# Key sums on halves of TensorE's columns, and a new ranking in a hand-made planner: linear attention and two MLPs on one core

## The chip, the cores and the metric

The kernel runs on one core of a Trainium2 chip. The metric is the device time of one execution in microseconds. The measurement of the kernel before is the median of 3 runs, 954.39 us (953.98 to 955.47).

## The reference, cut to what matters

The inputs are q, k, v of shape (4 batches, 8 heads, 576 tokens, 64), omega of 128 x 64, and the weights of two MLPs (512 to 2048 and back).

```python
def phi(x):
    h = x @ omega.T - sum(x * x) / 2
    return exp(h - max(h)) / sqrt(128)
q_p, k_p = phi(q * 64**-0.25), phi(k * 64**-0.25)
kv = einsum('bhsm,bhsd->bhmd', k_p, v)          # the key sums
z = sum(k_p, axis=2)
out = (q_p @ kv) / (q_p @ z + 1e-6)             # per batch and head
x = out as (2304 tokens, 512)
h = x @ w_in;  g = max(h, 0) + alpha * min(h, 0);  x = g @ w_out
h = x @ w2_in; g = 0 if h <= -1, h if h >= 1, else (h + 1)**2 / 4;  out = g @ w2_out
```

All of it is float32.

## The kernel before, in words

**Attention.** The 32 heads are worked on as 16 pairs of two heads of one batch. 576 tokens are 4 tiles of 128 (NJ = 4) and 64 last tokens, and the last tokens of both heads of a pair share one tile. For a pair, `features` (L344) multiplies keys and then queries with omega: a head has 64 features of input, so that the two heads use the two halves of TensorE's rows (L361). `last_features` (L367) does the last tokens (L373). `exponentials` (L329) takes the maximum on VectorE (L336) and 128 x 128 exponentials on ScalarE (L339). `key_sums` (L377) multiplies the keys' features with the values and a column of ones: one matmul for the last tokens with 130 moving columns (L388), then eight with 65 (L395), all into one PSUM bank; each float32 matmul is two passes in the trace. `transposed` (L432) transposes the queries' features, `quotients` (L467) multiplies them with the key sums (L473, or three products for pairs from 6 on), and `back` (L490) divides (L482 to L523) and writes x, the MLP's input.

**MLPs.** Tokens stand in four groups: one batch of 512 main tokens each, and in the fourth the 256 last tokens of all batches too. For each MLP, each group and each of 16 blocks of 128 hidden features there is a unit: 2 x 4 x 16 = 128 units in a row. A unit multiplies x with the first weights into a bank h (`hidden`, L673), applies the activation (`activate`, L644: L652 and L653 in the first MLP, L656 to L658 in the second) and multiplies with the second weights into the banks y (`project`, L682). Every product is three matmuls (L243 to L245) of a rounded part and a rest: `hi_of` (L225, ScalarE or VectorE) makes the rounded part, `lo_of` (L232) subtracts it. So the weights have a split for each unit (`split_weights`, L300: w_hi on ScalarE, w_lo on GpSimd), x one for each group (`split_x`, L626: x_hi and x_lo, 512 wide for main tokens and 256 wide for the last ones) and g one for each unit (L664, L665). The order of TensorE is: hidden of unit i + 1, then project of unit i.

**Words.** The weights come as 64-bit numbers. `convert` (L253) loads 512 KB into a word buffer (three of them, L251 and L257) and makes float32 in five steps on ScalarE, GpSimd and VectorE (L265 to L273). The first MLP's weights are converted during group 0, at most five units ahead; those of the second from the time when attention has given back its memory (`attended`, L608, event "late").

**What sets the order.** Nothing is scheduled by a compiler. `Plan` (L38) runs all streams in a simulated time when the kernel is built: each step names an engine and a charge in ns, and the planner emits the step that can start first; among those that start at the same time, the one of the lowest rank:

```python
return (start, s.pe_rank if engine == "pe" else s.rank, s.ready), engine, ns, emit
```

Each engine then executes in that order, and semaphores do the waiting. A rank decides only between steps that could start at the same time. Before, attention has rank 3 plus its batch (and ranks below 0 on TensorE), conversions of the first MLP 4.5, of the second 20, splits of weights 3.5, the MLPs, activations, x's splits and `finish` 0, and loads of attention's inputs about -100. `mlps` (L737) adds x's splits of the next group, all of them, with the first unit of a group; they wait there until x's parts are free (main tokens: when the last unit has used them; last tokens: these are used by group 3 alone).

Of the kernel before, what the change touches and what calls it, by code (L numbers as in the profile page):

```python
# [11 lines left out]
U32 = mybir.dt.uint32  # L12
# [134 lines left out]


def _pool_one(n, emit, handicap=0.0):
    return "pool", 80 + n, emit, handicap  # L150


def _pe(ns, emit):
    return "pe", ns, emit
# [7 lines left out]
def favor_attention_two_mlps(  # L162
# [20 lines left out]
    nc = tc.nc  # L183
# [13 lines left out]
    NE = NF // 2  # L197
    AHEAD = 5
    N_FULL = 6
    WARM = 18  # L200
    ROWS_NS = 264

    const = ctx.enter_context(tc.tile_pool(name="const", bufs=1))
    wpool = ctx.enter_context(tc.tile_pool(name="w", bufs=NF))
# [6 lines left out]

    plan = Plan()
    events = {}

    def ev(*key):
        return events.setdefault(key, Event())

    def done(*key):
        plan.set(ev(*key))
# [28 lines left out]
        return 3 * max(109.0, 13.5 + n / 2.4)  # L248


    raws = Tokens([0, 1, 2])  # L251

    def convert(dst, src, key):  # L253

        n = dst.shape[1]
        yield raws
        raw = stage_p.tile([P, 2 * n], U32, tag="raw", name="raw", bufs=3)  # L257
        yield _dma(P * n * 8, lambda: nc.sync.dma_start(raw, src))
        f = raw.bitcast(F32).rearrange("p (n t) -> p n t", t=2)[:, :, 1]
        h = raw.bitcast(U16).rearrange("p (n t) -> p n t", t=4)[:, :, 1]  # L260
        low, e = (raw.rearrange("p (n t) -> p n t", t=2)[:, :, t] for t in range(2))
        d = dst.bitcast(U32)

        yield [
            _act(n, lambda: nc.scalar.activation(f, f, AF.Copy, scale=2.0**-112)),  # L265
            _pool_one(n, lambda: nc.gpsimd.tensor_scalar(f, f, 2.0**-112, 0.0, ALU.mult, ALU.add), 300),
        ]
        yield _act(n, lambda: nc.scalar.activation(low, h, AF.Copy, scale=2.0**-13))
        yield _dve_fast(n, lambda: nc.vector.tensor_scalar(d, e, 3, None, ALU.logical_shift_left))  # L269
        yield _pool(n, lambda: nc.gpsimd.tensor_tensor(d, d, low, ALU.add))  # L270
        yield _dve_two(
            n,
            lambda: nc.vector.scalar_tensor_tensor(  # L273
                d, e, 0x80000000, d, ALU.bitwise_and, ALU.bitwise_or
            ),
        )
        plan.put(raws, 0)
        done("w", *key)
# [4 lines left out]
    def load_weights(l, src):  # L283
        for f in range(NF):
            if l == 0:
                yield ev("unit", f - AHEAD)
            if l == 1 and f < NE:
                yield ev("late")
                w = late["pool"].tile([P, 2, DM], F32, tag="w", name="w2", bufs=NE)
            else:  # L290
                yield w_slots
                w = wpool.tile([P, 2, DM], F32, tag="w", name="w")
            weights[l, f] = w
            for a in range(2):
                plan.add(convert(w[:, a, :], src[f, :, a * 2 * DM : (a + 1) * 2 * DM], (l, f, a)), (4.5, 20)[l])

    part_slots = [Tokens([0, 1]) for _ in range(2)]
    parts = {}
# [1 line left out]
    def split_weights(a):  # L300
        for i, (l, g, f) in enumerate(units):
            yield part_slots[a]
            yield ev("w", l, f, a)
            w = weights[l, f][:, a, :]
            hi = parts_p.tile([P, DM], F32R, tag=f"wh{a}", name="w_hi")
            lo = parts_p.tile([P, DM], F32R, tag=f"wl{a}", name="w_lo")
            yield hi_of(hi, w, 3000)
            yield lo_of(lo, w, hi, ("pool",))
            parts[i, a] = hi, lo
            done("part", i, a)  # L310
            if l == 0 and g == len(groups) - 1:
                if ev("split", f).at is not None:
                    plan.put(w_slots, 0)
                done("split", f)


    free_banks = Tokens(["y0", "y1", "y2", "y3", "a0", "a1"])
# [59 lines left out]
    def key_sums(pool, kf, lf, vm, vl, pair):  # L377
        for key in ("k0", "k1", "l"):
            yield ev(key, pair)
        yield kv_slots  # L380
        kv_hi = pool.tile([M, 2, 2 * D], F32R, tag="kvh", name="kv_hi", bufs=2)
        kv_lo = pool.tile([M, 2, 2 * D], F32R, tag="kvl", name="kv_lo", bufs=2)
        kvs[pair] = kv_hi, kv_lo
        tag = yield free_banks
        kv = bank(tag)

        def products():
            nc.tensor.matmul(  # L388
                kv[:, : 2 * (D + 1)], lf[:, 0, :], vl.rearrange("p h d -> p (h d)"), start=True, stop=False
            )  # L390
            for h in range(2):
                o = kv[:, h * (D + 1) : (h + 1) * (D + 1)]
                for j in range(NJ):
                    end = h == 1 and j == NJ - 1
                    nc.tensor.matmul(o, kf[:, 2 * j + h, :], vm[:, h, j, :], start=False, stop=end)  # L395

        yield _pe(216 * (2 * NJ + 1), products)
        plan.put(k_slot, 0)
        plan.put(v_slots, 0)
        if pair + 2 < B * NP:  # L400
            plan.add(load_values(pair + 2), pair - 97.5)
        done("kv sums", pair)

        kv3 = kv[:, : 2 * (D + 1)].rearrange("m (h d) -> m h d", h=2)
        z_hi, z_lo = (
            a.rearrange("m h d -> m (h d)")[:, D : 3 * D].rearrange("m (h d) -> m h d", h=2)
            for a in (kv_hi, kv_lo)
        )
        z = kv3[:, :, D : D + 1].to_broadcast([M, 2, D])
        cs = [slice(h * D, (h + 1) * D) for h in range(2)]  # L410

        one = pair < N_FULL

        def his():
            for h in range(2):
                o = kv_hi[:, h, cs[h]]
                nc.scalar.activation(o.bitcast(F32) if one else o, kv3[:, h, :D], AF.Copy)
            nc.scalar.activation(z_hi.bitcast(F32) if one else z_hi, z, AF.Copy)

        def los():  # L420
            for h in range(2):
                o = kv_hi[:, h, cs[h]].bitcast(F32)
                nc.vector.tensor_tensor(kv_lo[:, h, cs[h]], kv3[:, h, :D], o, ALU.subtract)
            nc.vector.tensor_tensor(z_lo, z, z_hi.bitcast(F32), ALU.subtract)

        yield "act", 370, his
        if not one:
            yield "dve", 472, los
        give(tag)
        done("kv", pair)  # L430
# [36 lines left out]
    def quotients(kv_hi, kv_lo, qh, ql, den, num, i, h, pair):  # L467
# [11 lines left out]
        done("n", pair, i, h)  # L479
        own, other = (slice(0, D), slice(D, 2 * D))[:: 1 - 2 * h]  # L480

        yield _dve(SH, lambda: nc.vector.transpose(den[own, c], n[other, :SH]))  # L482
        yield [
            _act(SH, lambda: nc.scalar.copy(num[own, c], n[own, :SH]), 0),
            _dve(SH, lambda: nc.vector.tensor_copy(num[own, c], n[own, :SH]), 50),
# [4 lines left out]
    def back(pool, qh, ql, b, hp, pair):  # L490
# [6 lines left out]
        num = pool.tile([P, S], F32, tag="num", name="num")  # L497
        for i in range(2):
            for h in range(2):
                plan.add(quotients(kv_hi, kv_lo, qh, ql, den, num, i, h, pair), 3 + b, b - 7)  # L500
        for i in range(2):
            for h in range(2):
                yield ev("den", pair, i, h)
# [5 lines left out]
            nc.vector.tensor_scalar(inv, squares[:, :, 0], EPS, None, ALU.add)  # L509
            nc.vector.reciprocal(inv, inv)  # L510

        yield "dve", 130 + 7.3 * NS, invert
        spread = inv.unsqueeze(2).to_broadcast([P, NS, 32])
        yield _dve(S, lambda: nc.vector.transpose(squares, spread))
        ends = [
            (x[b][:, hp, :], num[:, :SM], den[:, :SM]),
            (x[B][:, hp, b * SL : (b + 1) * SL], num[:, SM:], den[:, SM:]),
# [38 lines left out]
    def attend(pool):  # L556
        for pair in range(B * NP):
            b, hp = divmod(pair, NP)
            r = (3 + b, b - 7)
            yield ev("kq", pair, -1 if pair == 0 else 0)  # L560
            yield split_slot
            xt, vm, vl = loaded.pop(pair)
# [174 lines left out]
    def mlps():  # L737
        ys = {}
        for i in range(-1, NU):
            if i + 1 < NU:  # L740
                l, g, f = units[i + 1]
                if f == 0:
                    n = i + 1 + NF
                    if n < NU:
                        nl, ng, _ = units[n]
                        for b in groups[ng]:
                            for c in range(KC):
                                plan.add(split_x(nl, b, c), 0)
                    if l == 0:
                        for b in groups[g]:  # L750
                            plan.add(second_input(b), 0)
                yield ev("part", i + 1, 0)
                for b in groups[g]:
                    tag = yield h_banks
                    h = bank(tag)
                    for c in range(KC):
                        yield ev("xs", l, b, c)
                        yield hidden(i + 1, b, c, h)
                        if f == NF - 1:
                            plan.put(xs_slots[b // B, c], 0)  # L760
                    plan.add(activate(i + 1, b, h, tag), 0)
                plan.put(part_slots[0], 0)
            if i < 0:
                continue
# [10 lines left out]
            for b in groups[g]:  # L775
# [4 lines left out]
                for c in range(n // P if l else KC):  # L780
# [3 lines left out]
                    y, tag = ys[b, c // per]  # L784
                    yield project(i, b, c, y)
                    if f == NF - 1 and c % per == per - 1:
                        plan.add(finish(l, b, c, y, tag, tokens), 0)
                plan.put(g_slots[k], 0)
                gs.pop((i, b))
            plan.put(part_slots[1], 0)  # L790
# [51 lines left out]
    def setup():  # L842
        yield "act", 300, constants

    plan.add(setup(), 0)
    plan.add(load(alpha_sb, alpha, ("alpha",)), 0)
    for f in range(-AHEAD, 0):
        done("unit", f)
    plan.add(attend(pool), 3, -10)
    plan.add(attended(), 0)  # L850
    for l in range(2):
        plan.add(load_weights(l, (w1, w2)[l]), (4.5, 20)[l])
    for a in range(2):
        plan.add(split_weights(a), 3.5)
    for b in groups[0]:
        for c in range(KC):
            plan.add(split_x(0, b, c), 0)
    plan.add(mlps(), 0)
    plan.run()

# [46 lines left out]
```

## Time and profile before

| | |
|---|---|
| median of 3 runs | 954.39 us |
| the profiled execution | 956.27 us |
| its span, first to last instruction | 954.4 us |
| TensorE busy | 931.8 us (98%) |
| VectorE busy | 557.9 us (58%) |
| ScalarE busy | 515.8 us (54%) |
| GpSimd busy | 453.6 us (48%) |
| mean granted TensorE clock | 0.995 |

PE is TensorE, PEld its weight loads, DVE VectorE, ACT ScalarE, POOL GpSimd, SP SyncE. The span of the profiled execution is 1.87 us less than its time. Matmuls overlap in the trace: what a matmul costs in a row of matmuls is the distance of two starts, not its own duration. "L395" is line 395 of the kernel; lines 225 to 245 are helpers, where the names of the tiles tell who called.

### The profile page before, as it was taken

How to read it: one execution, taken by the hardware profiler on the slowest of the kernel's cores; microseconds unless marked ns; L12 is line 12 of the kernel's file. 1: busy time of each engine (PE TensorE's matmuls, PEld its weight loads, DVE VectorE, ACT ScalarE, POOL GpSimd, SP SyncE). 2: the span in 40 equal slices, each digit the busy share in tenths (PEclk: the TensorE clock that was granted, in tenths of full speed). 3: DMA queues.
4: the chain of work that ended last, by engine and by line, in shares of the span. 5: the costliest groups of instructions: out<-in, count | busy, mean ns of one | idle time of the engine just before them, and what ended most of it. 6: DMA issues, size and time to landing. Idle time of an engine off the chain costs nothing.

```text
span 954.4 us, 13551 instructions
## 1 busy us (share of the span) xinstructions
PE 931.8 (98%) x4908; PEld 776.5 (81%) x4908; DVE 557.9 (58%) x944; ACT 515.8 (54%) x1102; POOL 453.6 (48%) x375
## 2 busy tenths in 40 slices
PE   7898999999999999999999999999999999999997
PEld 6677877788888888888888888888887888888886
DVE  4899878885655777777753533453336334534342
ACT  6987777765555654654432354454445445533443
POOL 0544657653333587756743344444443444333330
PEclk9999999999999999999999999999999999999999
DMA  6544434411300023303300000010001000100002
GB/s 184 165 142 131 150 124 155 148 38 38 104 1 1 1 97 116 114 28 133 133 23 1 1 1 1 1 45 0 1 1 45 1 0 1 45 1 1 1 1 66
DMA packets 33858, 53.36 MB, mean 56 GB/s; under 512 B 20992, under 2 KB 21120, under 8 KB 33792
## 3 DMA queue, kind: packets, MB, share of 16 engines
q1 hardware_dynamic: 33632, 52.45, 16.7%
q8 instruction: 38, 0.62, 0.3%
q14 instruction: 28, 0.23, 0.1%
q10 hardware_dynamic: 160, 0.07, 0.0%
HBM read 47.78 MB, written 4.72 MB: 55 GB/s over the span
## 4 chain that ended last, share of the span: by engine, by line
PE 88%; DVE 6%; ACT 4%; issue 1%; DMA 0%; POOL 0%; ACTq 0%; DVEq 0%; POOLq 0%
PE h L243 13%; PE h L245 13%; PE h L244 13%; PE y L243 12%; PE y L245 12%; PE y L244 12%; PE a L243 2%; PE a L361 2%; PE a L245 2%; PE a L244 2%; PE a L395 2%; DVE nm L336 1%; PE a L443 1%; ACT kf L339 1%; DVE x_lo L237 1%
## 5 line engine op out<-in xcount | busy, mean ns | idle before, releaser
L238 POOL TENSOR_TENSOR w_lo<-w,w_hi 128x512 fp32r<-128x512 f32 x256 | 335.2, 1311 | 383.2 <-ACT w_hi L227 379.8
L227 ACT ACTIVATE w_hi<-w 128x512 fp32r<-128x512 f32 x256 | 161.6, 632 | 219.4 <-PE h L244 152.1
L243 PE MATMUL h<-x_hi,w_hi 128*128 128x512 f32 (+1 forms) x640 | 240.3, 376 | 0.0
L245 PE MATMUL h<-x_hi,w_lo 128*128 128x512 f32 (+1 forms) x640 | 236.4, 369 | 0.8 <-POOL w_lo L238 0.8
L244 PE MATMUL h<-x_lo,w_hi 128*128 128x512 f32 (+1 forms) x640 | 236.7, 370 | 0.0
L245 PEld LDWEIGHTS h<-x_hi,w_lo 128*128 128x128 f32 x640 | 121.0, 189 | 22.1 <-POOL w_lo L238 1.5
L243 PEld LDWEIGHTS h<-x_hi,w_hi 128*128 128x128 f32 x640 | 121.2, 189 | 21.7 <-DVE g_lo L236 0.4
L244 PEld LDWEIGHTS h<-x_lo,w_hi 128*128 128x128 f32 x640 | 121.1, 189 | 19.7 <-DVE x_lo L237 0.5
L227 ACT ACTIVATE g_hi<-h 128x512 fp32r<-128x512 f32 (+1 forms) x160 | 89.0, 556 | 83.1 <-DVE h L658 46.6
L236 DVE TENSOR_TENSOR g_lo<-h,g_hi 128x512 fp32r<-128x512 f32 (+1 forms) x160 | 100.2, 634 | 52.0 <-ACT g_hi L227 49.8
L656 DVE TENSOR_SCALAR t<-h 128x512 f32<-128x512 f32 x80 | 51.0, 638 | 135.3 <-PE h L245 133.2
L270 POOL TENSOR_TENSOR w<-w,raw 128x512 uint32<-128x512 uint32 x64 | 85.8, 1343 | 52.9 <-DVE w L269 19.2
L243 PE MATMUL y<-g_hi,w_hi 128*128 128x512 f32 x256 | 103.0, 402 | 0.1
L245 PE MATMUL y<-w_hi,g_lo 128*128 128x512 f32 x256 | 100.2, 391 | 2.3 <-DVE g_lo L236 2.3
L243 PE MATMUL y<-w_hi,g_hi 128*128 128x512 f32 x256 | 100.3, 392 | 0.0
L244 PE MATMUL y<-w_lo,g_hi 128*128 128x512 f32 x256 | 100.3, 392 | 0.0
L244 PE MATMUL y<-g_lo,w_hi 128*128 128x512 f32 x256 | 100.1, 391 | 0.0
L245 PE MATMUL y<-g_hi,w_lo 128*128 128x512 f32 x256 | 100.0, 391 | 0.0
L652 DVE TENSOR_SCALAR t<-h,alpha_sb 128x512 f32<-128x512 f32 x80 | 55.6, 694 | 64.7 <-PE h L245 63.0
L657 ACT ACTIVATE t<-t,half 128x512 f32<-128x512 f32 x80 | 54.5, 681 | 62.1 <-DVE t L656 62.1
L658 DVE TENSOR_TENSOR h<-h,t 128x512 f32<-128x512 f32 x80 | 51.5, 644 | 49.5 <-ACT t L657 49.5
L273 DVE SCALAR_TENSOR_TENSOR w<-raw,w 128x512 uint32<-128x512 uint32 x64 | 59.0, 928 | 8.8 <-POOL w L270 8.7
(115 smaller groups left out, 1308.0 us busy)
## 6 DMA issues: line engine op xcount, KB each, us to landing
raw<-w SPq DMA_DIRECT2D x64, 512.0 KB, 3.7
kq<-kq SPq DMA_DIRECT2D x15, 576.0 KB, 4.6
vm<-v SPq DMA_DIRECT2D x16, 256.0 KB, 3.0
out<-x SPq DMA_DIRECT2D x16, 256.0 KB, 2.0
vl<-v SPq DMA_DIRECT2D x32, 16.0 KB, 2.7
out<-x SPq DMA_DIRECT2D x4, 128.0 KB, 2.3
kq<-kq SPq DMA_DIRECT2D x1, 320.0 KB, 3.1
kq<-kq SPq DMA_DIRECT2D x1, 256.0 KB, 2.7
```

Of the source, the lines that this page charges most:

```text
L227: ops = [_act(n, lambda: nc.scalar.activation(hi, src, AF.Copy))]
L236: "dve": _dve(n, lambda: nc.vector.tensor_tensor(*args), bias),
L238: "pool": _pool(n, lambda: nc.gpsimd.tensor_tensor(*args)),
L243: nc.tensor.matmul(out_, wh, mh, start=first, stop=False)
L244: nc.tensor.matmul(out_, wh, ml, start=False, stop=False)
L245: nc.tensor.matmul(out_, wl, mh, start=False, stop=last)
L270: yield _pool(n, lambda: nc.gpsimd.tensor_tensor(d, d, low, ALU.add))
L273: lambda: nc.vector.scalar_tensor_tensor(d, e, 0x80000000, d, ALU.bitwise_and, ALU.bitwise_or),
L652: yield _dve(n, lambda: nc.vector.tensor_scalar(tn, hn, 0.0, a, ALU.min, ALU.mult))
L656: yield _dve(n, lambda: nc.vector.tensor_scalar(tn, hn, -1.0, 1.0, ALU.max, ALU.min))
L657: yield _act(n, lambda: nc.scalar.activation(tn, tn, AF.Square, bias=half[:, 0:1], scale=0.5), 50)
L658: yield _dve(n, lambda: nc.vector.tensor_tensor(hn, hn, tn, ALU.max))
```

## The change

Six things, of which the diff is the core:

- The key sums' matmuls write 64 of the 128 features each: twice as many matmuls, with stationary tiles of 64 columns, and both halves in turn. The planner charges 1480 ns for a pair in place of 1944.
- The word buffers are four in place of three.
- Ranks: x's splits, activations, `finish` and the constants get -10. Attention gets the number of the unit by which it is due, conversions and weight splits that of the unit which needs them. A weight's split is a stream of its own.
- x's splits of the last tokens are added with the ninth unit of the group before, in place of the first.
- Charges: the projections 298 ns in place of 264 per tile, the transposes of `quotients` and `back` and the inverse a fixed 508, 710 and 480 ns in place of 367, 670 and 261, and L266's alternative on GpSimd 60 ns more.
- On TensorE attention's rank is the pair less 50, in place of the batch less 7.

```diff
-    return "pool", 80 + n, emit, handicap
+    return "pool", 140 + n, emit, handicap
...
+    RAWS = 4
     WARM = 18
-    ROWS_NS = 264
+    ROWS_NS = 298
+    KV_NS = 1480
...
+    URGENT = -10
+
+    def attention_rank(pair):
+        b, hp = divmod(pair, NP)
+        return hp - 8 if b == 0 else NF * (b - 1) + NF // NP * (hp + 1)
+
+    def weight_rank(i):
+        return i - 5.5 if i < 2 else i
...
-    raws = Tokens([0, 1, 2])
+    raws = Tokens(range(RAWS))
...
-                plan.add(convert(w[:, a, :], src[f, :, a * 2 * DM : (a + 1) * 2 * DM], (l, f, a)), (4.5, 20)[l])
+                i = l * len(groups) * NF + f
+                plan.add(convert(w[:, a, :], src[f, :, a * 2 * DM : (a + 1) * 2 * DM], (l, f, a)), weight_rank(i))
...
+            plan.add(split_weight(a, i, weights[l, f][:, a, :], hi, lo), weight_rank(i) - 0.1)
...
-            nc.tensor.matmul(
-                kv[:, : 2 * (D + 1)], lf[:, 0, :], vl.rearrange("p h d -> p (h d)"), start=True, stop=False
-            )
+            halves = [slice(i * M // 2, (i + 1) * M // 2) for i in range(2)]
+            for r in halves:
+                o = kv[r, : 2 * (D + 1)]
+                nc.tensor.matmul(o, lf[:, 0, r], vl.rearrange("p h d -> p (h d)"), start=True, stop=False)
             for h in range(2):
-                o = kv[:, h * (D + 1) : (h + 1) * (D + 1)]
                 for j in range(NJ):
                     end = h == 1 and j == NJ - 1
-                    nc.tensor.matmul(o, kf[:, 2 * j + h, :], vm[:, h, j, :], start=False, stop=end)
-
-        yield _pe(216 * (2 * NJ + 1), products)
+                    for r in halves:
+                        o = kv[r, h * (D + 1) : (h + 1) * (D + 1)]
+                        nc.tensor.matmul(o, kf[:, 2 * j + h, r], vm[:, h, j, :], start=False, stop=end)
+
+        yield _pe(KV_NS, products)
...
-        yield _dve(SH, lambda: nc.vector.transpose(den[own, c], n[other, :SH]))
+        yield "dve", 508, lambda: nc.vector.transpose(den[own, c], n[other, :SH])
...
-                plan.add(quotients(kv_hi, kv_lo, qh, ql, den, num, i, h, pair), 3 + b, b - 7)
+                plan.add(quotients(kv_hi, kv_lo, qh, ql, den, num, i, h, pair), attention_rank(pair), pair - 50)
...
-            r = (3 + b, b - 7)
+            r = (attention_rank(pair), pair - 50)
...
+                n = i + 1 + NF
+                if f in (0, NF // 2) and n < NU:
+                    nl, ng, _ = units[n]
+                    for b in groups[ng]:
+
+                        if (f == 0) == (b < B):
+                            for c in range(KC):
+                                plan.add(split_x(nl, b, c), URGENT)
                 if f == 0:
-                    n = i + 1 + NF
-                    if n < NU:
-                        nl, ng, _ = units[n]
-                        for b in groups[ng]:
-                            for c in range(KC):
-                                plan.add(split_x(nl, b, c), 0)
...
-                    plan.add(activate(i + 1, b, h, tag), 0)
+                    plan.add(activate(i + 1, b, h, tag), URGENT)
...
-                        plan.add(finish(l, b, c, y, tag, tokens), 0)
+                        plan.add(finish(l, b, c, y, tag, tokens), URGENT)
```

## Rows read from the trace of the kernel before

**Rows 1.** The page's first part: busy us and share of the span.

```profile
PE 931.8 (98%) x4908; PEld 776.5 (81%) x4908; DVE 557.9 (58%) x944; ACT 515.8 (54%) x1102; POOL 453.6 (48%) x375
```

**Rows 2.** Stretches: length, busy time by engine (instructions), granted clock, DMA share, GB/s.

```profile
0.00:58.00 58.00, 49.00 (x390) 39.00 (x390) 37.99 (x80) 46.20 (x147) 20.13 (x32) 0.97 0.57 166
58.00:205.00 147.00, 140.81 (x833) 114.00 (x832) 124.86 (x230) 107.80 (x282) 87.14 (x71) 0.99 0.41 135
...
547.00:720.00 173.00, 173.00 (x771) 143.49 (x771) 71.92 (x103) 85.54 (x138) 81.78 (x63) 1.00 0.02 7
720.00:735.00 15.00, 12.66 (x49) 9.94 (x48) 11.53 (x18) 7.28 (x14) 5.15 (x4) 0.89 0.19 72
```

**Rows 3.** Timeline of PE at 725 us: start, us, instruction [idle before <-releaser].

```profile
725.58 0.39 PE L244 MATMUL y<-w_lo,g_hi 128*128 128x512 f32 x1
728.30 0.50 PE L245 MATMUL y<-w_hi,g_lo 128*128 128x512 f32 x1 [2.34 <-DVE g_lo L236]
```

**Rows 4.** Timeline of DVE, 721 to 728 us.

```profile
721.74 1.45 DVE L237 TENSOR_TENSOR x_lo<-x,x_hi 128x512 fp32r<-128x512 f32 x1
...
723.71 1.53 DVE L229 CAST x_hi<-x 128x256 fp32r<-128x256 f32 x2
725.16 2.48 DVE L237 TENSOR_TENSOR x_lo<-x,x_hi 128x256 fp32r<-128x256 f32 x4
727.57 0.68 DVE L236 TENSOR_TENSOR g_lo<-h,g_hi 128x512 fp32r<-128x512 f32 x1
```

**Rows 5.** The chain that ended last, after the hole: start, us on it.

```profile
729.52 0.42 PE y L243
...
732.50 0.43 PE h L244
```

**Rows 6.** Timeline of DVE one group earlier.

```profile
634.70 1.45 DVE L237 TENSOR_TENSOR x_lo<-x,x_hi 128x512 fp32r<-128x512 f32 x1
...
637.43 0.69 DVE L236 TENSOR_TENSOR g_lo<-h,g_hi 128x512 fp32r<-128x512 f32 x1 [0.67 <-ACT g_hi L227]
```

**Rows 7.** Timeline of DVE in the middle of group 2, second MLP.

```profile
773.36 0.69 DVE L656 TENSOR_SCALAR t<-h 128x512 f32<-128x512 f32 x1 [1.84 <-PE h L245]
774.90 0.70 DVE L658 TENSOR_TENSOR h<-h,t 128x512 f32<-128x512 f32 x1 [0.85 <-ACT t L657]
```

**Rows 8.** The chain that ended last, one pair's key sums (pair 14).

```profile
275.36 0.23 PE a L388 x2
275.59 1.73 PE a L395 x16
277.32 0.18 PE a L243
```

**Rows 9.** Timeline of PE around one L361 group in halves of the rows.

```profile
262.33 0.40 PE L245 MATMUL h<-x_hi,w_lo 128*128 128x512 f32 x1
262.65 1.16 PE L361 MATMUL a<-om,kq 64*128 64x128 f32 x16
...
264.08 0.39 PE L244 MATMUL h<-x_lo,w_hi 128*128 128x512 f32 x1
```

**Rows 10.** The chain that ended last, early: a pair's key sums.

```profile
22.70 1.73 PE a L395 x16
```

**Rows 11.** Waits of PE between 58 and 205 us, first and last of seven.

```profile
PE a L361 <- ACT kf L339: 1.8, 1, 1.8
...
PE y L473 <- DVE num L485: 0.3, 1, 0.3
```

**Rows 12.** Timeline of POOL: the last product of pair 7.

```profile
125.33 0.33 POOL L523 TENSOR_TENSOR x<-num,den 128x64 f32<-128x64 f32 x1
```

**Rows 13.** Timeline of PE: the first matmul of group 1, first MLP.

```profile
204.66 0.39 PE L243 MATMUL h<-x_hi,w_hi 128*128 128x512 f32 x1
```

**Rows 14.** Timeline of POOL: the last product of the last pair.

```profile
321.99 0.32 POOL L523 TENSOR_TENSOR x<-num,den 128x64 f32<-128x64 f32 x1
```

**Rows 15.** Timeline of PE: the first matmul of group 3, first MLP.

```profile
414.25 0.39 PE L243 MATMUL h<-x_hi,w_hi 128*128 128x512 f32 x1
```

More of the change, by code (lines that the diff above doesn't have):

```diff
@@ L256, in convert @@
         yield raws
-        raw = stage_p.tile([P, 2 * n], U32, tag="raw", name="raw", bufs=3)
+        raw = stage_p.tile([P, 2 * n], U32, tag="raw", name="raw", bufs=RAWS)
         yield _dma(P * n * 8, lambda: nc.sync.dma_start(raw, src))
@@ L303, in split_weights, with split_weight @@
             yield ev("w", l, f, a)
-            w = weights[l, f][:, a, :]
             hi = parts_p.tile([P, DM], F32R, tag=f"wh{a}", name="w_hi")
             lo = parts_p.tile([P, DM], F32R, tag=f"wl{a}", name="w_lo")
-            yield hi_of(hi, w, 3000)
-            yield lo_of(lo, w, hi, ("pool",))
             parts[i, a] = hi, lo
[L310 to L314, printed above, removed]
+            plan.add(split_weight(a, i, weights[l, f][:, a, :], hi, lo), weight_rank(i) - 0.1)
+    def split_weight(a, i, w, hi, lo):
+        l, g, f = units[i]
+        yield hi_of(hi, w, 3000)
+        yield lo_of(lo, w, hi, ("pool",))
+        done("part", i, a)
+        if l == 0 and g == len(groups) - 1:
+            if ev("split", f).at is not None:
+                plan.put(w_slots, 0)
+            done("split", f)
     free_banks = Tokens(["y0", "y1", "y2", "y3", "a0", "a1"])
@@ L510, in invert @@
             nc.vector.reciprocal(inv, inv)
-        yield "dve", 130 + 7.3 * NS, invert
+        yield "dve", 480, invert
         spread = inv.unsqueeze(2).to_broadcast([P, NS, 32])
-        yield _dve(S, lambda: nc.vector.transpose(squares, spread))
+        yield "dve", 710, lambda: nc.vector.transpose(squares, spread)
         ends = [
@@ L843, in setup @@
         yield "act", 300, constants
-    plan.add(setup(), 0)
+    plan.add(setup(), URGENT)
     plan.add(load(alpha_sb, alpha, ("alpha",)), 0)
@@ L851, in favor_attention_two_mlps @@
     for l in range(2):
-        plan.add(load_weights(l, (w1, w2)[l]), (4.5, 20)[l])
+        plan.add(load_weights(l, (w1, w2)[l]), 0)
     for a in range(2):
-        plan.add(split_weights(a), 3.5)
+        plan.add(split_weights(a), 0)
     for b in groups[0]:
         for c in range(KC):
-            plan.add(split_x(0, b, c), 0)
+            plan.add(split_x(0, b, c), URGENT)
     plan.add(mlps(), 0)
```

## The prediction

> **What bounds the kernel now.** I read the engines' busy time first. TensorE is busy for 931.8 us of a span of 954.4 us [rows 1], so the kernel gains only where TensorE gets less work, gets no hole, or keeps its clock. The profiled execution took 956.27 us: its span and 1.87 us around it. The median of the runs shown, 954.39 us, is 1.88 us less. I work out differences on the profiled execution and take them from the median. What a measurement can tell from no change is about 0.2%, 1.9 us.
>
> Next, the stretches [rows 2]. From 547 to 720 us TensorE is busy all the time. From 58 to 205 us, where group 0 of the first MLP and half of the attention share the engines, it lacks 6.2 us (147.0 less 140.8), and the granted clock of 0.99 costs 1.7 us more. VectorE is at 85% there (124.9 of 147). Before 58 us TensorE has only attention and lacks 9 us. The last striking stretch is 720 to 735 us: 2.3 us short, and a clock of 0.89. Outside these the only waits are at the very end, where the last output leaves.
>
> Then the hole at 725 us. A matmul that reads g_lo starts at 728.30 where the one before it started at 725.58 [rows 3]; at the usual 0.23 us it would have started at 725.81, so 2.49 us are lost. VectorE made that g_lo late, at 727.57, since two casts and four subtractions of 256 columns, from 723.71 on, stood ahead of it [rows 4]: those are the splits of the last tokens for group 3, issued when group 2 begins and its own splits are still going on. Behind the hole eight matmuls of 512 columns take 0.42 to 0.43 us in place of 0.23 us [rows 5], which is the lower of the two clock levels, 1.2 GHz: eight times 0.2, and a little at the edge, 1.7 us. The hole costs 4.2 us in all.
>
> **Splits moved: 4.2 us gained.** The change adds the last tokens' splits half a group earlier, eight units before. No instruction is added. At the boundary one group earlier there are no such splits, and the same sequence of VectorE, up to the subtraction at 634.70, is followed by g_lo at 637.43 [rows 6], 2.8 us after that subtraction started; at 725 us it was 5.8 us (727.57 less 721.74). The gap to the matmul was 2.49 us, so 3 us less is enough. In the new place a unit of group 2 leaves VectorE idle for 1.84 us ahead of t and 0.85 us ahead of h [rows 7], and a unit lasts 5.44 us (24 matmuls at 0.227). Four subtractions of 0.62 us and a cast or two, 3.9 us by [rows 4], spread over two units' gaps. What is queued behind a split is then g_lo of that unit; by the same pattern the matmul that reads it starts 1.9 us after g_lo is done, and that is the cover. If it is gone, each split in a row costs 0.6 us and the hole comes back smaller: I take 4.2 us, and 2 us as the low end. Above it nothing more can be won here.
>
> **Key sums by halves: 5 us gained.** A pair's key sums are now L388 in two passes, 0.23 us, and L395 in sixteen, 1.73 us, with 0.05 us more at the next matmul [rows 8]: 2.0 us. A pass of 65 columns takes 0.108 us, hardly less than one of 130 at 0.115, so the moving columns don't set it; what the passes have in common is a stationary tile of 128 columns. The change makes 36 passes of 18, each with a stationary tile of half as many columns. No row shows column halves. The nearest are the row halves of L361 [rows 9]: sixteen passes with 64 rows each. From the start of the matmul before them to the start of the second one behind is 1.75 us; less two matmuls at 0.227 this is 1.30 us. Sixteen passes one after another at the 0.108 us above would be 1.73 us, so they run by twos: eight steps of 0.11 us are 0.90 us, and entering and leaving the halves costs the other 0.40 us. By that model the key sums are 16 steps of 0.054 us (half the stationary columns; 65 moving columns also take no more, half of 0.11), 2.5 steps of 0.11 us for the 130 columns, and 0.40 us: 1.54 us, which I round up to 1.6 us, 0.4 us less for each pair. The bounds: 1.0 us less (half of today's, no cost at the edges), and 2.4 us more (36 passes at 0.11 and the edges). I take the model, since L361 is the same engine in halves next to the same matmuls.
>
> How many pairs count? TensorE is the bound from 58 us on, where 11 of the 16 pairs have their key sums: 4.4 us. The first five lie in the stretch where TensorE waits for ScalarE and VectorE; there the key sums stand on the chain that ended last, at 1.73 us [rows 10], and some of their 0.4 us reach the end. 5 us in all, between 4.4 and 6.4 by the model; with the bound, 11.
>
> **Order: 3 us gained.** What is left is the hand-made planner. Its charges for the transposes, the inverse, L265 on GpSimd and the projections go up, the key sums' down; the conversions and splits of weights are ranked by the unit that reads them, the attention pairs 4 to 15 by the unit by which they are due, and activations ahead of all but loads. Before, pairs 4 to 7 came ahead of every conversion and pairs 8 to 15 behind them. Now pair 4 comes behind units 0 to 3, pair 7 behind all sixteen. So in the stretch from 58 to 205 us weights arrive sooner and less attention is squeezed in; it moves to where VectorE has room. What this can give back is what TensorE lacks there: seven rows of waits, from 1.8 us for an exponential to 0.3 us [rows 11], 6.2 us in all, and the 1.7 us of clock. The fourth word buffer lets SP issue a fourth 512 KB load of words ahead; only 0.8 us of those waits are for a weight's w_lo, so I give it no term of its own; the SP queue behind it holds loads of later pairs, which the planner still issues first. The gain is between 8 us and, should the new order lose as much as half of that at other places, a loss of 4 us. I take 3 us, somewhat above the middle of 2: work that is ready while attention waits is what was missing.
>
> **Sum.** 4.2 + 5 + 3 = 12.2 us. 954.39 less 12.2 is 942.2 us.
>
> **Rivals.** *The halves run one after the other.* Then 32 passes of 0.054 us, four of 0.11 and the 0.40 us are 2.57 us, 0.57 us more than now, 6.3 us over 11 pairs; with the hole and the order it is 954.39 - 4.2 - 3 + 6.3 = 953.5 us. For it: both halves need all 128 rows, while L361's share none. Against it: the output partitions are disjoint, as L361's rows are. 10%.
>
> *No load under a running matmul.* If a half's stationary tile could not be loaded while a matmul of the same rows runs, a pass would be 0.054 us of load and 0.054 us of moving columns: 32 at 0.108, four at 0.164 and 0.40 us, 4.5 us, 2.5 us more than now, 27 us over 11 pairs: 974 us. The Trainium skill, page "TensorE: Matmul & The Clock Gate", section "Part 3: Packing small matmuls — row/col tiling", says that weight loads overlap running matmuls only where the row group differs, which speaks against this change. L395 as it stands speaks against the strict form: all its passes use the same rows and still follow each other at 0.108 us, the time of a pass of twice the columns [rows 8]. 3%.
>
> *Attention just in time*, the rival on the slower side. Pair 7 is now done at 126 us [rows 12] and group 1 begins at 204.66 [rows 13]; the last pair is done at 322 us [rows 14] and group 3 begins at 414.25 [rows 15]. The new ranks make these pairs due at the unit that reads them, behind its weights. If a pair is done only after the previous group's last matmul, TensorE idles for the lateness, one for one, and then pays 1.7 us of clock as at 728 us. With 10 us at two of the boundaries it is 23 us: 965 us. It decides against the change from about 12 us in all. Against it: margins of 79 and 92 us, and a planner that leaves no engine idle for a rank. 7%.
>
> *The change does not do what it says*: the splits are added earlier but the planner places them at the same boundary, or in other gaps where they make the same hole, and order and halves cancel: 954 us. 3%.
>
> **Numbers.** The forecast has 77%: 74 of them faster, 2 within 0.2%, 1 slower (its terms at their bad ends). Halves one after the other: 4, 4 and 2. No overlap: 3 slower. Just in time: 1 same, 6 slower. No effect: 2 same, 1 slower. Faster 0.78, same 0.09, slower 0.13. The range begins at 934 (4.2, 8 for the key sums, between model and bound, and 8 for the order: 20 us less) and ends at 955, which takes in the halves one after the other; outside are the two slow rivals and the tails, some 2 in 10.
>
> **What would show it.** Right: no TensorE wait for g_lo near the start of group 2 of the second MLP and a granted clock of 1.0 there; splits of 256 columns eight units earlier; key sums of about 1.6 us from the first pass to the next matmul; less TensorE idle between 58 and 205 us; attention ending later than 322 us but ahead of group 3. Wrong: key sums of 2 us or more; TensorE waits at the starts of groups 1 to 3; or a first unit that starts well after 58 us, since four pairs have to be through before any MLP matmul and I gave that stretch nothing but the key sums.

## The result, and the profile after

The changed kernel takes 942.59 us (median of 4 runs, 941.48 to 943.21), beside 954.93 us for the kernel before on the same chip: a ratio of 0.9869, with a 95% interval of 0.9855 to 0.9883. It is 12.3 us faster; 12.2 us were forecast. The profiled execution took 942.46 us with a span of 940.7 us, 13.7 us shorter than the one before.

The page's first part (busy us, share of the span, instructions) answers to [rows 1]: TensorE is still busy for 98%, so the kernel is bound as it was, with 11.6 us less of TensorE's busy time. The 288 more matmul records are the key sums' halves (18 for each of 16 pairs).

```profile
PE 920.2 (98%) x5196; PEld 760.6 (81%) x5196; DVE 549.5 (58%) x927; ACT 521.5 (55%) x1120; POOL 453.7 (48%) x374
```

The same stretches as in [rows 2]; the columns are the same too. From 58 to 205 us TensorE now lacks 3.7 us (147.00 less 143.30) in place of 6.2, at full clock. The boundary of [rows 3] lies at 713 us now; from 547 to 735 us TensorE lacks nothing, so the hole is gone, and the clock is 1.00. New are small lacks, 0.5 us from 205 to 327 us and 1.3 us from 327 to 414 us, where there was none, and before 58 us it lacks 1.0 us more. The stretches don't hold the same work: group 1 begins at 176.73 us in place of 204.66.

```profile
0.00:58.00 58.00, 48.01 (x482) 35.48 (x482) 40.13 (x78) 48.60 (x156) 24.52 (x36) 1.00 0.65 193
58.00:205.00 147.00, 143.30 (x916) 114.29 (x918) 118.76 (x209) 106.44 (x265) 93.09 (x73) 1.00 0.37 117
205.00:327.00 122.00, 121.55 (x822) 98.06 (x816) 80.36 (x142) 72.56 (x195) 47.65 (x41) 1.00 0.14 42
327.00:414.00 87.00, 85.66 (x425) 70.88 (x425) 64.55 (x99) 48.30 (x91) 56.99 (x47) 1.00 0.18 61
...
547.00:720.00 173.00, 173.00 (x765) 143.25 (x764) 76.25 (x108) 86.96 (x140) 82.00 (x64) 1.00 0.03 10
720.00:735.00 15.00, 15.00 (x68) 12.40 (x67) 5.72 (x9) 6.59 (x11) 7.78 (x6) 1.00 0.07 28
```

The kernel before, from 205 to 414 us:

```profile
205.00:327.00 122.00, 122.00 (x700) 100.49 (x699) 76.45 (x144) 66.99 (x171) 50.77 (x46) 1.00 0.09 28
327.00:414.00 87.00, 87.00 (x385) 72.09 (x384) 67.31 (x94) 51.31 (x88) 65.43 (x49) 1.00 0.28 97
```

Over the whole span TensorE idles for 20.5 us (940.7 less 920.2), before for 22.6 us (954.4 less 931.8). Without the hole's 2.3 us it was 20.3. Outside the hole, idle time has moved and has not become less.

One pair's key sums in the timeline of PE (start, us from the first start to the last end, instruction) answer to [rows 8]. The stationary tile is written 128*64. From the last ordinary matmul's start (275.21) to the second matmul behind (277.07) it is 1.86 us; in the kernel before the same distance is 2.38 us for pairs 10 to 15 (274.97 to 277.34 in the rounded rows of pair 14, below). A pair gains 0.515 us.

```profile
275.21 0.39 PE L259 MATMUL h<-x_hi,w_lo 128*128 128x512 f32 x1
275.53 0.44 PE L410 MATMUL a<-vl,lf 128*64 128x130 f32 x4
275.80 1.10 PE L416 MATMUL a<-vm,kf 128*64 128x65 f32 x32
276.84 0.40 PE L257 MATMUL a<-qh,kv_hi 128*128 128x288 f32 x1
277.07 0.29 PE L258 MATMUL a<-ql,kv_hi 128*128 128x288 f32 x1
```

```profile
274.97 0.40 PE L245 MATMUL h<-x_hi,w_lo 128*128 128x512 f32 x1
...
277.34 0.29 PE L244 MATMUL a<-ql,kv_hi 128*128 128x288 f32 x1
```

The last tokens' splits in the second MLP, in DVE's timeline: they stand at 756 to 760 us, with the ninth unit of group 2, and fill gaps like those of [rows 7]. No matmul waits for a g_lo there.

```profile
756.38 0.48 DVE L243 CAST x_hi<-x 128x256 fp32r<-128x256 f32 x2
757.14 0.69 DVE L250 TENSOR_TENSOR g_lo<-h,g_hi 128x512 fp32r<-128x512 f32 x1 [0.27 <-ACT g_hi L241]
757.74 2.52 DVE L251 TENSOR_TENSOR x_lo<-x,x_hi 128x256 fp32r<-128x256 f32 x4
```

And the small new lack, in PE's timeline: the first unit of group 3 of the first MLP waits for an x_lo, 1.34 us as idle time. From 404.42 to 406.14 is 1.72 us where 0.23 us would do, so 1.5 us are lost.

```profile
404.42 0.39 PE L257 MATMUL h<-x_hi,w_hi 128*128 128x512 f32 x1
406.14 0.50 PE L258 MATMUL h<-x_lo,w_hi 128*128 128x512 f32 x1 [1.34 <-DVE x_lo L251]
```

### The profile page after: what moved, and what is told of

The parts are those of the page before. It is cut to its first block, busy times and chain, and to the rows that moved or that the text cites. A ratio compares the mean times of both kernels' runs of the same rounds, so it can differ in the third digit from the quotient of the medians.

```text
span 940.7 us, 14096 instructions
## 1 busy us (share of the span) xinstructions
PE 920.2 (98%) x5196; PEld 760.6 (81%) x5196; DVE 549.5 (58%) x927; ACT 521.5 (55%) x1120; POOL 453.7 (48%) x374
## 4 chain that ended last, share of the span: by engine, by line
PE 89%; DVE 4%; ACT 4%; issue 1%; DMA 0%; POOL 0%; ACTq 0%
PE h L258 14%; PE h L259 14%; PE h L257 14%; PE y L257 12%; PE y L258 12%; PE y L259 12%; PE a L257 2%; PE a L379 2%; PE a L259 2%; PE a L258 2%; ACT kf L357 1%; PE a L416 1%; PE a L464 1%; ACT qf L357 1%; DVE x_lo L251 1%; DVE nm L354 1%
## 5 line engine op out<-in xcount | busy, mean ns | idle before, releaser
L259 PEld LDWEIGHTS y<-g_hi,w_lo 128*128 128x128 f32 x256 | 48.1, 188 | 10.5
```

Of the source, the lines that this page charges most:

```text
L259: nc.tensor.matmul(out_, wl, mh, start=False, stop=last)
```

## The experiments

Twelve kernels, each timed beside the kernel before (954.5 to 954.8 us). The ratio is to the kernel before. The last column is a difference of medians that were measured apart; by the ratios, old charges lose 3.7 us, three buffers gain 1.8 and held gains 0.9.

| kernel | us, median | ratio (95%) | against the changed kernel |
|---|---|---|---|
| changed | 942.59 | 0.9869 (0.9855 to 0.9883) | |
| full columns | 949.93 | 0.9944 (0.9929 to 0.9959) | +7.3 |
| halves apart | 955.77 | 1.0007 (0.9996 to 1.0018) | +13.2 |
| splits at boundary | 945.18 | 0.9895 (0.9877 to 0.9912) | +2.6 |
| old ranks | 945.26 | 0.9898 (0.9882 to 0.9913) | +2.7 |
| old charges | 945.27 | 0.9908 (0.9893 to 0.9924) | +2.7 |
| three buffers | 939.18 | 0.9850 (0.9833 to 0.9867) | -3.4 |
| nudged | 945.37 | 0.9902 (0.9884 to 0.9920) | +2.8 |
| three nudged | 952.08 | 0.9974 (0.9963 to 0.9985) | +9.5 |
| held | 940.95 | 0.9860 (0.9842 to 0.9877) | -1.6 |
| three held | 938.49 | 0.9832 (0.9818 to 0.9846) | -4.1 |
| before + halves only | 950.58 | 0.9952 (0.9935 to 0.9968) | |
| before + splits only | 951.76 | 0.9973 (0.9962 to 0.9984) | |

The kernels differ in their mean granted clock too: 0.998 to 0.999 in the executions of the changed kernel, 0.995 to 0.997 in those of full columns and old charges, 0.995 to 0.996 in nudged, 0.990 to 0.994 in three nudged, and 1.000 in three held. A mean that is lower by 0.001 over 950 us makes up to 1 us (less where TensorE idles at the half clock). So part of these differences is clock.

### What the column halves are worth

**Full columns**: the changed kernel with the matmuls of before, at the same charge.

```diff
-            for r in halves:
-                nc.tensor.matmul(kv[r, : 2 * (D + 1)], lf[:, 0, r], ..., start=True, stop=False)
+            nc.tensor.matmul(kv[:, : 2 * (D + 1)], lf[:, 0, :], ..., start=True, stop=False)
...
-                    for r in halves:
-                        nc.tensor.matmul(o, kf[:, 2 * j + h, r], vm[:, h, j, :], start=False, stop=end)
+                    nc.tensor.matmul(o, kf[:, 2 * j + h, :], vm[:, h, j, :], start=False, stop=end)
```

> The changed kernel with the key sums' matmuls of before (9 of 128 columns for each pair); planner's charge and so the order of everything are as in the changed kernel. Theory (TensorE is the bound, halves run side by side): the 0.515 us that a pair's key sums now take less come back, for the 11 pairs after the first unit 5.7 us, up to 8.2 us if all 16 count: 948 to 951 us. Rival (the new order is what gained, the halves' gain is lost in waits): at most 2 us more, under 945 us.

949.93 us, 7.3 us more. The rival falls. At 0.515 us that is 14 of the 16 pairs, but up to 2 us of it can be clock (a mean of 0.9965 beside 0.9988), and without them it is 10 pairs. The first matmul of the first unit, with full columns and then in the changed kernel:

```profile
59.13 0.61 PE L257 MATMUL h<-x_hi,w_hi 128*128 128x512 f32 x1
```

```profile
57.02 0.61 PE L257 MATMUL h<-x_hi,w_hi 128*128 128x512 f32 x1
```

So 2.1 of the 6.7 us between the two spans (947.4 and 940.7 us) lie ahead of that unit. Of these, 1.4 us lie behind the start of the second pair's key sums (22.02 and 21.29 us), where the clock is 1.00 in both: the early pairs, before the first unit, count too.

**Halves apart**: the same 36 passes, but all of one half first.

```diff
             for r in halves:
                 o = kv[r, : 2 * (D + 1)]
                 nc.tensor.matmul(o, lf[:, 0, r], ..., start=True, stop=False)
-            for h in range(2):
-                for j in range(NJ):
-                    for r in halves:
+                for h in range(2):
+                    for j in range(NJ):
```

> The changed kernel with all 9 matmuls of the first column half, then all 9 of the second, in place of the two halves in turn; charge and order of the rest unchanged. Theory (neighbours on different column halves run side by side): passes follow one another at 0.056 us with 65 columns and 0.11 us with 130, 2.2 us of passes in place of 1.31, so 0.9 us more for each pair, 10 us over 11 pairs and 15 over 16: 952 to 957 us. Rival (the gain is only that a stationary tile of 64 columns loads faster, and the order of the halves is of no matter): within 1 us of the changed kernel, 942 to 944 us.

955.77 us, 13.2 us more than in turn and as slow as the kernel before. The timeline of PE of this kernel, one pair:

```profile
286.01 0.39 PE L259 MATMUL h<-x_hi,w_lo 128*128 128x512 f32 x1
286.33 0.44 PE L410 MATMUL a<-vl,lf 128*64 128x130 f32 x2
286.61 0.92 PE L415 MATMUL a<-vm,kf 128*64 128x65 f32 x13
...
287.48 1.20 PE L415 MATMUL a<-vm,kf 128*64 128x65 f32 x17
288.61 0.40 PE L257 MATMUL a<-qh,kv_hi 128*128 128x288 f32 x1
288.85 0.29 PE L258 MATMUL a<-ql,kv_hi 128*128 128x288 f32 x1
```

From 286.01 to 288.85 is 2.84 us in place of 1.86. The 36 passes take 2.28 us (286.33 to 288.61), in turn 1.31 us (275.53 to 276.84), and of those the 32 short ones 1.04 us, 0.033 us each. The single records of the trace show how. With one half after the other, a pass of 65 columns starts 0.058 us behind the one before it; with full columns it was 0.112 us. In turn, the passes of the two halves start 0.007 us apart, and the next two 0.058 us later. So a stationary tile of half the columns alone only halves the short pass, for twice as many passes; the passes of 130 columns, at 0.11 us, don't become shorter by it, and the edges come on top: 2.84 us for a pair where full columns take 2.38, and 5.8 us for the kernel (955.77 beside 949.93). The gain is in the turns: neighbours on different halves run side by side.

Loads and matmuls of the changed kernel lie in the same time; all engines' timeline from 275.85 to 276.05 us has these two rows (the ends of matmuls are modelled):

```profile
275.80 0.46 PE L416 MATMUL a<-vm,kf 128*64 128x65 f32 x10
275.80 0.38 PEld L416 LDWEIGHTS a<-vm,kf 128*64 128x64 f32 x10
```

The Trainium skill, page "TensorE: Matmul & The Clock Gate", section "Part 3: Packing small matmuls — row/col tiling", holds that weight loads overlap running matmuls only where the row group differs. These halves use all rows, and the trace speaks against it: 0.033 us for each pass, loads included.

**Before + halves only** puts the same edit into the kernel before, in its old order.

> The kernel before with the halved key sums alone, charge 1944 and order as before. Theory: 5.7 us less (11 pairs at 0.515) to 8.2 us less (16 pairs): 946 to 949 us against 954.4. Rival (in the old order TensorE waits more in the first 205 us and takes the gain back): under 3 us less.

950.58 us, 4.2 us less, between theory and rival: 8 pairs' worth. Its key sums are as short as in the changed kernel (1.86 us by the measure above for the last pairs). The rest went into waits: from 58 to 205 us TensorE is busy for 2.9 us less than in [rows 2], and before 58 us for 1.4 us less. The longest of its waits there are below (waiting, releaser, us in total, times, longest); against the kernel before the second has grown from 1.0 us and the fourth is new.

```profile
PE a L361 <- ACT kf L339: 1.8, 1, 1.8
PE a L373 <- DVE kv_lo L426: 1.5, 1, 1.5
PE a L243 <- ACT lf L339: 1.3, 1, 1.3
PE a L243 <- DVE kv_lo L426: 1.3, 2, 1.1
```

Who waits for kv_lo waits for what VectorE makes from the key sums: a shorter key sum that is queued in a fixed order only lets the next matmul wait for VectorE.

### What the moved splits are worth

**Splits at boundary**: the changed kernel with them back at the first unit.

```diff
-                        if (f == 0) == (b < B):
+                        if f == 0:
```

> The changed kernel with the last tokens' splits added with the first unit of the group before, as they were. Theory (these splits stand ahead of a g_lo on VectorE when group 2 of the second MLP begins): the hole of some 2.5 us and the half clock behind it come back, 4.2 us more: 947 us. Rival (with activations ranked as high as splits the hole would have gone anyway): within 1 us, 942 to 944 us.

**Before + splits only**: the kernel before with that condition, nothing else.

> The kernel before with the last tokens' splits added with the ninth unit of the group before, all else as before. Theory: the 2.5 us hole at 725 us goes, and the half clock behind it where a run has it: 2.5 to 4.2 us less than before, 950.5 to 952.2 us. Rival (the splits make the same hole in their new place): within 1 us of before.

2.6 us and 2.8 us (951.76 against 954.52). The hole is there in the one and gone in the other, so the rivals fall, but 4.2 us was too much. The stretches around the hole, of the splits at the boundary and then of the halves alone (which keep the hole too):

```profile
710.00:730.00 20.00, 17.66 (x71) 14.05 (x70) 12.87 (x20) 9.28 (x17) 7.75 (x6) 0.91 0.14 53
```

```profile
715.00:735.00 20.00, 17.66 (x78) 14.31 (x77) 14.51 (x22) 10.75 (x19) 7.73 (x6) 1.00 0.14 53
```

Both lack the same 2.34 us. In the one execution the clock falls behind it (0.91 of 20 us is 1.8 us), in the other it does not. The idle time is paid in each execution, the half clock only in some.

### What order, charges and buffers are worth

**Old ranks, old charges, three buffers**: the changed kernel with one of them set back.

```diff
-    URGENT = -10
+    URGENT = 0
...
-        return hp - 8 if b == 0 else NF * (b - 1) + NF // NP * (hp + 1)
+        return 3 + b
...
-        return i - 5.5 if i < 2 else i
+        return 4.5 if i < 64 else 20
...
-            plan.add(split_weight(...), weight_rank(i) - 0.1)
+            plan.add(split_weight(...), 3.5)
...
-            r = (attention_rank(pair), pair - 50)
+            r = (attention_rank(pair), b - 7)
```

> The changed kernel with all ranks of before (attention 3 plus its batch, conversions 4.5 and 20, weight splits 3.5, activations, splits and finish 0, on TensorE the batch less 7); halves, buffers, charges and the place of the last tokens' splits as in the changed kernel. Theory (the ranks are what gained the order's 3 us): pairs 4 to 7 crowd group 0's weights again, TensorE is less busy between 58 and 205 us by 3 us or more, 945 to 948 us. Rival (the ranks only move work, and cost at group 3 what they gain in group 0): 941 to 944 us.

```diff
-    return "pool", 140 + n, emit, handicap
+    return "pool", 80 + n, emit, handicap
...
-    ROWS_NS = 298
-    KV_NS = 1480
+    ROWS_NS = 264
+    KV_NS = 1944
...
-        yield "dve", 508, lambda: ...
+        yield _dve(SH, lambda: ...)
-        yield "dve", 480, invert
+        yield "dve", 130 + 7.3 * NS, invert
-        yield "dve", 710, lambda: ...
+        yield _dve(S, lambda: ...)
```

> The changed kernel with the planner's charges of before (projections 264, key sums 1944, transposes, inverse and the GpSimd scaling), everything else as changed. Theory (charges move single instructions by less than a us): 942 to 945 us. Rival (the planner's truer clock is what keeps TensorE from waiting for attention's exponentials and maxima): 946 us or more, with more waits for L339's or L482's successors.

```diff
-    RAWS = 4
+    RAWS = 3
```

> The changed kernel with three word buffers. Theory (weights were seldom late in the trace of before, so the fourth buffer has no term): within 1 us of the changed kernel, 942 to 944 us. Rival (the fourth buffer is what lets group 0's weights arrive in time): TensorE lacks 6 us again between 58 and 205 us, and 945 us or more.

Ranks and charges each look like 2.7 us, the ranks at the low end of what the theory said, the charges a little above theirs and short of the rival. The fourth buffer looks like a loss of 3.4 us, which neither side had said. (By the ratios it is 1.8 us, and the intervals of three and four buffers overlap.) And the price of the ranks is not in every execution: two of the five took 942.9 us, like the changed kernel, at a clock of 0.999 and 1.000, the others 945.3 to 945.5 us at 0.997 and 0.998. Three prices for parts that share one order, one of them of the wrong sign, asked for a control.

**Nudged, three nudged**: one charge moved by 4 ns, with four and with three buffers.

```diff
-    ROWS_NS = 298
+    ROWS_NS = 302
```

> A control: the changed kernel with one charge moved by 4 ns (projections 302 in place of 298 per tile), which changes single places in the order and nothing else. Theory (ranks, charges and buffers each have a price of their own): within 1 us of the changed kernel, 941.5 to 943.6 us. Rival (any change of the planner's clock shuffles the order in the first 330 us, and the 2.7 to 3.4 us seen for ranks, charges and the fourth buffer are as much luck of the order as merit): it moves by 1.5 us or more, either way.

> The same control with three word buffers. Theory (the fourth buffer itself costs 3.4 us): it stays at 938 to 940.5 us, below the four buffers with the same charge. Rival (luck of the order): three and four buffers with this charge differ by another amount than 3.4 us, or the other way.

Four buffers lose 2.8 us by it, three lose 12.9 us (939.18 to 952.08). The rival holds: a change that has no price of its own moves the time as much as ranks, charges or the buffer did, and more. In the stretch from 58 to 205 us the rows of old ranks, nudged and three nudged read, in this order:

```profile
58.00:205.00 147.00, 140.35 (x984) 110.64 (x983) 126.18 (x224) 109.80 (x283) 93.08 (x73) 1.00 0.40 125
```

```profile
58.00:205.00 147.00, 141.24 (x926) 112.52 (x925) 116.93 (x213) 105.88 (x265) 90.67 (x72) 0.99 0.39 119
```

```profile
58.00:205.00 147.00, 137.54 (x867) 108.53 (x866) 119.04 (x210) 103.83 (x253) 89.44 (x71) 0.97 0.39 121
```

With the old ranks TensorE lacks 6.7 us there, as in the kernel before, and so far the reason given for the ranks is right. But that execution is one of the two at 942.9 us: it lacks 3.0 us more here, 1.7 us more over the whole span (941.1 less 918.9 is 22.2, beside 20.5), and takes no longer. And a nudge alone makes the lack 5.8, or 9.5 us and 0.97 of the clock. Where those 9.5 went, in PE's timeline and for the stretch around it, of three nudged:

```profile
73.62 0.48 PE L466 MATMUL a<-ident,lf 128*128 128x128 f32 x1 [5.49 <-ACT lf L357]
73.75 0.78 PE L257 MATMUL y<-g_hi,w_hi 128*128 128x512 f32 x1
74.33 0.63 PE L258 MATMUL y<-g_lo,w_hi 128*128 128x512 f32 x1
74.75 0.63 PE L259 MATMUL y<-g_hi,w_lo 128*128 128x512 f32 x1
...
79.02 0.50 PE L258 MATMUL y<-g_lo,w_hi 128*128 128x512 f32 x1
79.36 0.39 PE L259 MATMUL y<-g_hi,w_lo 128*128 128x512 f32 x1
```

```profile
60.00:80.00 20.00, 13.14 (x79) 9.84 (x77) 16.93 (x28) 12.13 (x32) 9.38 (x8) 0.74 0.39 126
```

One transpose of the last tokens' features is next in TensorE's order and waits 5.5 us for its exponential; whether the work behind it could have run is not shown. Behind the wait two matmuls of 512 columns start 0.42 us apart (74.33 to 74.75), the lower clock level, and at 79 us it is over: 5.4 us of work, half of which, 2.7 us, is lost to the clock. (The 0.74 also takes in idle time, in which a low clock loses nothing.)

### The wait at group 3, and a better version

**Held**: the second MLP's conversions wait until group 3 of the first has begun.

```diff
             if l == 0:
                 yield ev("unit", f - AHEAD)
+            elif f == 0:
+                yield ev("group 3")
...
+            if i == len(groups) * NF - NF:
+                done("group 3")
```

> The changed kernel with the second MLP's weight conversions held back until group 3 of the first MLP has begun. Theory (conversions on VectorE at the boundary are what makes x_lo late at 404 us, 1.5 us): that wait goes, 940.5 to 941.5 us. Rival (the splits alone fill VectorE there, or the conversions make a new wait in the second MLP): 942 us or more.

940.95 us, 1.6 us less, as the theory said, though by the intervals the two are not apart. The trace shows it: from 327 to 414 us TensorE is now busy without a gap, with VectorE at 48 us in place of 65. In this order, then, the conversions on VectorE were what made x_lo late.

```profile
327.00:414.00 87.00, 87.00 (x420) 72.62 (x417) 47.95 (x80) 36.25 (x67) 40.17 (x35) 1.00 0.00 1
```

But they need not be in the way. The nudged kernel keeps its conversions, has them on VectorE 5 us ahead of its group 3 (408.34 us), and TensorE has no gap either. The same stretch and DVE's timeline, of nudged:

```profile
327.00:414.00 87.00, 87.00 (x433) 72.56 (x433) 64.28 (x98) 51.15 (x95) 59.96 (x47) 1.00 0.19 61
```

```profile
403.20 2.39 DVE L287 SCALAR_TENSOR_TENSOR w<-raw,w 128x512 uint32<-128x512 uint32 x2
405.51 1.88 DVE L251 TENSOR_TENSOR x_lo<-x,x_hi 128x512 fp32r<-128x512 f32 x3
```

**Three held** has this edit and three buffers.

> Three word buffers and the conversions held back: the best of the versions seen, put together. Theory: the x_lo wait of 0.7 us at group 3 goes, 937.5 to 939.5 us. Rival: what moves the conversions moves another wait in, 940 us or more.

938.49 us, with four runs within 0.21 us: 16.1 us faster than the kernel before, and 4.1 us faster than the changed kernel, with intervals that don't touch. It is the best version seen. Of its three buffers the control above says that they may be luck, and three buffers alone, at 939.18 us, are not apart from it by the intervals. That the conversions must keep clear of a boundary is not shown, since those of nudged don't and cost nothing there.

## Why the prediction was right, and where it was not

**The sum** came out at 12.2 us against 12.3, but its terms did not come out one by one: 5 was 7.3 (up to 2 of them clock), 4.2 was 2.6, and 3 was the 2.4 that is left. That they meet within 0.1 us is luck.

**Key sums.** The model by L361's rows held: steps by twos at half the time (0.058 us where 0.054 was taken), and the edges. From the distance of 1.86 us, less what the two matmuls around would take (0.227 and 0.135), the key sums are 1.50 us; the model's own sum was 1.54 us, and rounding it up to 1.6 was the worse choice. (From the first pass to the next matmul, as the prediction's last paragraph names it, they are 1.31 us.) The edge shows at the entry (275.21 to 275.53, 0.32 us where 0.23 is usual) and at the exit (276.84 to 277.07, 0.23 us where 0.135 is), as at L361. The Trainium skill, page "TensorEngine Tiling (Array Packing)", section "Key Properties", says that a change of the tiling mode drains the engine. The rows agree, at under 0.4 us for both edges together. The term was also short in what the early pairs give: 0.6 us was taken, 1.4 us show. How much of the 7.3 us is clock stays open. The rivals of halves one after the other and of no overlap are refuted by the rows; what the first would have cost is what the halves apart cost, 0.46 us for a pair above full columns where it said 0.57.

**Splits.** The mechanism was right to the place and the unit. The mis-sized step was "1.7 us" of half clock, taken from one execution as if each paid it. 2.5 us of idle time and a part of the 1.7 fit the 2.6 and 2.8 us measured.

**Order.** This is the step that failed as an argument, though its 3 us landed: "Work that is ready while attention waits is what was missing". TensorE does lack 2.5 us less between 58 and 205 us than before, and with the old ranks that comes back. But as much came up elsewhere: outside the hole it idles for 20.5 us where it idled for 20.3. So the 2.4 us that are left are not idle time won; the rows show the clock in its place, 1.00 up to 205 us where it was 0.97 and 0.99, up to 3 us in the profiled executions as an estimate from these rows (0.03 of 58 us and 0.01 of 147 us). And a 4 ns nudge brings the lack back as the old ranks do, so no run here shows that the ranks, the charges or the buffer earn it rather than the order that happened to come out. The range of -4 to +8 us for this term was right in kind; 12.9 us for a nudge says that it was still too narrow. What the four parts of the order are worth beyond luck stays open.

**Just in time.** The rival did not decide, but it came closer than its 7%, and one of the prediction's signs of being wrong, TensorE waits at the starts of groups 1 to 3, did show, too small to decide: 0.67 us at group 1 and 1.34 us at group 3. These two rows, of GpSimd's and of PE's timeline, answer to [rows 12, 13]: pair 7 was done 79 us ahead of group 1 and is now done 4 us ahead of it (172.70 to the group's first matmul at 176.73), and x_lo is late by 0.67 us.

```profile
172.38 0.32 POOL L544 TENSOR_TENSOR x<-num,den 128x64 f32<-128x64 f32 x1
```

```profile
176.73 0.39 PE L257 MATMUL h<-x_hi,w_hi 128*128 128x512 f32 x1
177.79 0.50 PE L258 MATMUL h<-x_lo,w_hi 128*128 128x512 f32 x1 [0.67 <-DVE x_lo L251]
```

The last pair is done at 349 us, 54 us ahead of group 3 where it was 92. What cost 1.5 us at group 3 was not attention itself: its x was done, and the last subtractions for x_lo came late on VectorE, behind a conversion, at 404.30 us where the group had begun at 403.06:

```profile
398.51 1.52 DVE L283 TENSOR_SCALAR w<-raw 128x512 uint32<-128x512 uint32 x1
399.96 1.28 DVE L251 TENSOR_TENSOR x_lo<-x,x_hi 128x512 fp32r<-128x512 f32 x2
...
404.30 2.39 DVE L251 TENSOR_TENSOR x_lo<-x,x_hi 128x512 fp32r<-128x512 f32 x2
```

## What to carry to other kernels

Where the columns of the stationary tile, and not the moving columns, set the time of a pass (0.108 us with 65 and 0.115 us with 130 moving columns here), two halves of TensorE's columns in turn give back a quarter of it, but only in turn; one half after the other was 5.8 us slower than full columns. Price a hole by its idle time alone, and the half clock behind it by its share of executions. And where a planner writes the order at build time, nudge a charge by a few ns before giving a rank or a buffer credit: here that alone moved the time by 2.8 and 12.9 us, and all the ranks together by 2.7. And look at the idle time of the whole span: what one stretch wins, another may lose.

## What was not expected of the hardware

That the same idle time of 2.34 us leaves the clock at 1.00 in one execution and takes it to half in the next. That with three buffers a single wait, 2.3 us for ql near 304 us, shows the same: the clock over 20 us around it was 0.91 in the profile of three buffers and 1.00 in that of three held.

```profile
300.00:320.00 20.00, 17.46 (x91) 13.21 (x90) 13.95 (x21) 9.49 (x26) 7.74 (x7) 0.91 0.01 1
```

```profile
298.00:318.00 20.00, 17.48 (x97) 13.48 (x96) 15.18 (x23) 10.95 (x30) 8.86 (x7) 1.00 0.00 1
```

The four executions of three buffers are 939.13, 939.14, 939.22 and 941.91 us; the profiled one is the last, 2.7 us above the rest.
